# A list scheduler's durations, latencies and load rates replaced, with pauses counted between whole-array and tiled matmuls

## The chip, the cores and the metric

The kernel runs on one core of one Trainium2 chip. The metric is the device time of one execution in microseconds (us), the median of several runs. The engines are TensorE (PE), VectorE (DVE), ScalarE (ACT), GpSimd (POOL) and SyncE (SP, which issues all transfers here). Each takes its own instructions strictly in the order in which the program lists them, and waits for the others through semaphores.

## What is computed

Attention with rotary position codes over 4 batches, 8 heads, 576 positions and head size 64, and behind it a gated network on the 2304 tokens of width 512:

```python
q_rot, k_rot = (rotate(q), rotate(k))
scores = np.matmul(q_rot, k_rot.transpose(0, 1, 3, 2)) / np.sqrt(D)
attn = np.exp(scores - np.max(scores, axis=-1, keepdims=True))
attn = attn / (np.sum(attn, axis=-1, keepdims=True) + 1e-09)
x = np.matmul(attn, v).transpose(0, 2, 1, 3).reshape(B * S, H * D)
...
gate = 1.0 / (1.0 + np.exp(-(x @ w_gate)))      # 512 -> 1536
val = x @ w_val                                  # 512 -> 1536
return (gate * val @ w_out).astype(np.float32)   # 1536 -> 512
```

## The kernel before

Values that need more than 16 bits are held as a scaled float16 and a float16 remainder, and a product is three matmuls of such parts. The eight heads of a batch are four pairs `p`, one head on each half of the 128 partitions. A batch's 576 positions are worked in two halves `i` of 256 and 320 (`HALVES`), with five query tiles `t`: four of 128 and one of 64.

*Attention of batch 0* (`front`, `back`, lines 626 to 723) stays in float32. `front` makes the scores of a tile into a PSUM buffer of the pool `s` (two buffers, taken in turn), and DVE takes their maximum (L645); `back` makes the scores again with the maximum subtracted (L685, L690), ACT takes the exponential (L696), and PE weighs the values and sums (L707); DVE takes a slow reciprocal (L717).

*Attention of batches 1 to 3* (`attention`, `softmax`, `score_mm`, lines 562 to 624 and 725 to 758) works in tiles. PE makes the scores of a pair (batch 1: L572, float32 on half the rows of the array; batches 2 and 3: L584, float16 on the whole array, tile 4 on half the columns). DVE scales them out of PSUM with their extremum (L607), ACT takes the exponential with its sum (L612), two small DVE operations make the reciprocal of the sum (L615, L617), ACT and DVE write the weight as part and remainder (both by helpers, L360 and L366), SP issues a transposing transfer (L738), and when all tiles of a half are there PE multiplies with the values (L748, on half the columns). Rotation of keys and queries is done by DVE for batches 0 and 1 (L514 to L516) and by POOL for 2 and 3 (L521 to L525); for the latter the split keys and queries are copied into `stk` by eight small transfers a pair (L551 to L557).

*The network*: `hidden` (lines 789 to 819) makes, for each of twelve chunks `f` of 128 columns, gate and value by 12 matmuls each (L799), with tanh on ACT (L805) and the product on DVE (L809); `project` (lines 821 to 848) makes 36 matmuls of 512 columns for 128 tokens (L833). Its weights arrive as 64-bit floats and are decoded and split by ACT and DVE in the opening (L366 to L447).

*What sets the order.* Nothing is written in program order. Each step calls `Plan.add` with the engine and its cost in us, a rank, what it reads and writes, and for a transfer a time to landing. `Plan.order` (lines 92 to 201) then plays the program through: at every turn the engine that is free first takes, among the tasks that are ready by then, the one of the lowest rank, whether or not a more urgent one would be ready a little later. A task is ready when its predecessors are done; a result from another engine counts `HOP` later (lines 135 to 143), a transfer its share of one common `bus` and a latency (lines 187 to 190). POOL's tasks and the DVE operations with two SBUF inputs (`op2`) book a common `port` and don't overlap in the plan (lines 184 to 186). The pools `m` and `th` give out a buffer when a task is placed, the others in turn. The tasks are emitted in the order of their planned starts, so each engine's instruction stream is the plan's. Ranks are set in lines 866 to 934: batch `b`'s network has ranks `b` to `b + 1`, the attention of batch `b + 1` from 0.05 less; batch 0's attention starts at -2, the decoding of the input weights at -1.75.

The costs come from four functions (lines 209 to 222) and from constants at the call. A batch's ranks don't depend on them.

Of the kernel before, what the change touches and what calls it, by code (L numbers as in the profile page):

```python
# [58 lines left out]
class Plan:  # L59


    HOP = 0.2
# [5 lines left out]
    def add(self, where, rank, reads, writes, fn, land=0.0, port=False, also=()):  # L68
# [20 lines left out]
        self.tasks.append((where, rank, fn, land, port))  # L89
        self.preds.append(sorted(pre))  # L90

    def order(self):
# [34 lines left out]
        def release(n):  # L127
            for x in self.leases[n]:
                x.left -= 1
                if not x.left:  # L130
                    slots[x.pool][x.n] = max(done[m][1] + done[m][2] for m in x.users) + self.HOP
                    for m in parked.pop(x.pool, []):
                        offer(m)

        def offer(n):
            for e, _ in self.tasks[n][0]:
                t = 0.0
                for m in self.preds[n]:
                    e0, end, land = done[m]
                    t = max(t, end if e0 == e and not land else end + land + self.HOP)  # L140
# [7 lines left out]
        starts, bus, port = [], 0.0, 0.0  # L148
        while len(starts) < N:
# [32 lines left out]
            where, rank, fn, land, locks = self.tasks[n]  # L182
            cost = dict(where)[e]
            if e == "POOL" or (e == "DVE" and locks):
# [24 lines left out]
def c_dve(n, psum=False, two=False):  # L209
    return 0.07 + n / 960 + (0.08 if psum else 0) + (0.15 if two else 0)  # L210


def c_act(n):
    return 0.24 + n * 0.00087


def c_pool(n, two=False):
    return 0.16 + n * (0.0025 if two else 0.0011)


def c_pe(n):
    return n / 2250
# [3 lines left out]
def rope_attention_then_sigmoid_glu(ctx: ExitStack, tc: tile.TileContext, qk, v, w_in, w_out, tables, out):  # L226
# [88 lines left out]
    def mm(us, rank, reads, writes, fn):  # L315
        P.add((("PE", us),), rank, reads, writes, lambda _: fn())

    def tiny(rank, reads, writes, fn, us=0.18):
# [11 lines left out]
    def allmax(rank, src, n, where, reads):  # L330
# [7 lines left out]
        mm(0.15 * n, rank, reads + ["ident"], [Z], turn_up)  # L338
        tiny(rank, [Z], [("row", k)], lambda: V.tensor_reduce(
            out=row[0:1, 2 * k:2 * k + n], in_=at()[0:1, 0:128 * n].rearrange("p (j c) -> p j c", j=n), axis=AX.X,  # L340
            op=ALU.max), us=0.3)
        mm(0.15, rank, [("row", k), "ident"], [Z], lambda: T.matmul(
# [3 lines left out]
    def allsum(rank, src, n, where, reads):  # L346

        at, Z = where
        mm(0.4, rank, reads + ["zero"], [Z], lambda: T.matmul(at()[:, 0:n], lhsT=ones, rhs=src, start=True, stop=True))
# [36 lines left out]
    def w_in_chunk(f, rank):  # L386
# [12 lines left out]
        for g in range(2):  # L399
            op("ACT", c_act(512) + 0.08, rank, tok, [M, W], lambda E, g=g: A.activation(  # L400
# [16 lines left out]
    def w_out_decode(f, rank):  # L417
# [10 lines left out]
        op("ACT", c_act(512) + 0.08, rank, [tok], ["sink", "wob"], lambda E: A.activation(  # L428
# [21 lines left out]
    def values0(rank, step):  # L450
        raw = xt[0].rearrange("p c a n -> p c (a n)").bitcast(F32)
        todo = []
        for p in range(NP):
# [6 lines left out]
            op("ACT", c_act(S) + 0.12, rank, X, ["sink", ("vm", 0)], lambda E, p=p, o=o: A.activation(  # L460
# [18 lines left out]
    def values(b, rank, step):  # L479
# [3 lines left out]
        for p in range(NP):  # L483
            op("ACT", c_act(S) + 0.12, rank, X, ["sink", ("vm", b)], lambda E, p=p: A.activation(
# [11 lines left out]
    def keys_queries(b, p, rank):  # L496
# [34 lines left out]
        for m in range(2):  # L531
            op("ACT", c_act(S) + 0.12, rank, [X[m]], ["sink", M], lambda E, m=m: A.activation(
# [29 lines left out]
    def score_mm(b, p, t, heads, rank):  # L562

        n = slots[b, p][0]
        if b < NW:
            kT, qT = qk0[n][:, 0], qk0[n][:, 1]

            def both(rows, width, to):
# [7 lines left out]
            mm(0.66 * len(heads), rank, R, list(heads),  # L576
               lambda: both(t * 128, 128 if t < 4 else 64, to))
# [12 lines left out]
        else:  # L590
            h = heads[0]
            mm(8 * c_pe(288), rank, R[0] + R[1], [h], lambda: [
                one(e, h()[64 * e:64 * e + 64], 512, 64) for e in range(2)])

    def softmax(b, p, t, u, rank):
# [14 lines left out]
        for c, h in enumerate(heads):  # L610
            op("ACT", c_act(S) + 0.12, rank - 0.01, [("st", k, c)], [prs[c], ("su", k, c)],
# [5 lines left out]
        tiny(rank, [], [("rs", k)], lambda: V.reciprocal(st[:, k, 2, 0:n], st[:, k, 2, 0:n]), us=0.16)  # L617
# [8 lines left out]
    def front(p, i, z, rank):  # L626
# [4 lines left out]
        for x, t in enumerate(((0, 1), (2, 3, 4))[i]):  # L631
            for c in range(2 if t < 4 else 1):
# [10 lines left out]
                mm(0.57 if t < 4 else 1.1, rank, R, [k], direct)  # L643
# [26 lines left out]
    def back(p, i, z, rank):  # L670
# [7 lines left out]
        for j in range(5):  # L678
# [12 lines left out]
            mm(0.0023 * n, rank, R, [k], across)  # L691
# [3 lines left out]
            op("ACT", c_act(2 * n if j < 4 else n), rank - 0.01, [k], [("pt", w, j)],  # L695
# [13 lines left out]
        for js in ((0, 1), (2, 3, 4)):  # L709
            mm(len(js) * 0.0034 * n, rank - 0.02, [("pt", w, j) for j in js] + [("v16", p)], ["pv", U],  # L710
               lambda js=js: weigh(js))
# [5 lines left out]
        op("DVE", 0.1 + 0.0064 * n, rank - 0.02, [], [K], lambda E: V.reciprocal(t(), t()))  # L717
# [7 lines left out]
    def attention(b, p, i, rank, step):  # L725
        n = 0
        z = p % 2 if (b, i) == (0, 0) else i
        for t in ((0, 1), (4, 2, 3) if b % 2 else (2, 3, 4))[i]:
# [9 lines left out]
            transpose(rank, U, [("pt", z, j) for j in range(5)], 2.8 if w == 128 else 1.6, lambda u=u, n=n, w=w: Y.dma_start_transpose(  # L738
# [50 lines left out]
    def hidden(b, f, i, rank):  # L789
# [3 lines left out]
        if i == 0 and b == 0:  # L793
            op("ACT", 0.2, rank, [("vs", b), ("ws", f)], [("gsc", b, f)], lambda E: A.activation(
# [191 lines left out]
```

## Time and profile before

| | |
|---|---|
| median of 3 runs | 716.72 us (716.29 to 717.3) |
| span of the profiled execution, first to last instruction | 719.6 us |
| busy: PE, DVE, ACT, POOL | 672.3 (93%), 482.9 (67%), 437.0 (61%), 73.9 (10%) us |
| weight loads of PE (beside the matmuls) | 426.9 us (59%) |
| mean granted clock of PE | 0.974 of full speed |
| transfers | 89.38 MB, mean 124 GB/s |

The profile records the span of the profiled execution, and no time around it; the span is 2.9 us (0.4%) above the median of the runs without a profile. Busy time of PE is modelled to the end of a matmul's way through the array, so short pauses between two matmuls count as busy. A line of the profile such as L607 is a line of the kernel; L360 and L366 are helpers, told apart there by the tile that they write.

### The profile page before, as it was taken

To read this page: it belongs to the slowest core of one execution; us is meant where nothing else is said; L and a number is where in the kernel's file an instruction comes from. 1 tells how busy PE (TensorE), PEld (TensorE's weight loads), DVE (VectorE), ACT (ScalarE), POOL (GpSimd) and SP (SyncE) were. 2 spreads that over 40 slices of the span, in tenths; PEclk is the share of its full clock that TensorE was granted. 3 is DMA by queue.
4 is the path that set the end of the run, shared out by engine and by line. 5 is a ranking of instruction groups with operands and counts; after the bars stand their busy time and mean duration, and the time that the engine had idled before them with its cause. 6 is when DMAs were issued, how large, how long until landed. Compare 5 with 4: busy or idle time off the path is not lost.

```text
span 719.6 us, 12869 instructions
## 1 busy us (share of the span) xinstructions
PE 672.3 (93%) x4986; PEld 426.9 (59%) x4986; DVE 482.9 (67%) x1062; ACT 437.0 (61%) x885; POOL 73.9 (10%) x57
## 2 busy tenths in 40 slices
PE   1687889999999998998998899999999999999997
PEld 1343455565675455775564665578667756866753
DVE  5677676889888668877797886779938682311310
ACT  2583967796878866665776678577738663322320
POOL 0300000000303001133135001114000000000000
PEclk9996989999999999999998999999999999999999
DMA  9731305226364337664996559764544542000001
GB/s 348 315 125 62 133 41 209 93 92 215 122 163 99 96 96 178 161 165 87 203 210 142 105 126 231 166 159 118 126 110 117 90 109 79 1 15 16 1 15 30
DMA packets 145230, 89.38 MB, mean 124 GB/s; under 512 B 128912, under 2 KB 133648, under 8 KB 143248
## 3 DMA queue, kind: packets, MB, share of 16 engines
q1 hardware_dynamic: 145168, 88.56, 45.7%
q8 instruction: 39, 0.64, 0.4%
q14 instruction: 23, 0.19, 0.1%
HBM read 43.12 MB, written 4.72 MB: 66 GB/s over the span
## 4 chain that ended last, share of the span: by engine, by line
PE 85%; DVE 8%; ACT 3%; DMA 2%; issue 1%; SPq 0%; DVEq 0%; ACTq 0%
PE m L799 37%; PE m L833 20%; PE pv L748 6%; PE s L584 5%; PE s L641 3%; PE s L572 3%; PE pv L707 3%; PE s L690 2%; PE m L707 2%; DVE p L366 1%; PE s L685 1%; DVE p L607 1%; DMA stk<-in_qk_dram 1%; DMA pt<-p 1%; DVE m L645 1%
## 5 line engine op out<-in xcount | busy, mean ns | idle before, releaser
L799 PE MATMUL m<-xt,w 128*128 128x320 f16 (+1 forms) x2304 | 297.1, 287 | 2.3 <-ACT th L805 2.3
L799 PEld LDWEIGHTS <-w 128*128 128x128 f16 x2304 | 221.7, 98 | 74.3 <-issue 18.6
L833 PE MATMUL m<-wo,gt 128*128 128x512 f16 x648 | 146.4, 381 | 0.0
L612 ACT ACTIVATE p<-p,st 128x576 f32<-128x576 f32 x108 | 83.1, 770 | 52.0 <-DVE p L607 45.3
L833 PEld LDWEIGHTS <-gt 128*128 128x128 f16 x648 | 62.4, 98 | 74.2 <-issue 5.0
L366 DVE SCALAR_TENSOR_TENSOR p<-p,st,p 128x576 f16<-128x576 f32 x108 | 91.5, 874 | 20.5 <-ACT p L360 20.2
L809 DVE SCALAR_TENSOR_TENSOR th<-th,m 128x256 f32<-128x256 f32 (+1 forms) x96 | 43.1, 450 | 75.1 <-PE m L799 71.9
L360 ACT ACTIVATE p<-p,st 128x576 f16<-128x576 f32 x108 | 78.3, 763 | 10.6 <-DMA pt<-p 4.5
L360 ACT ACTIVATE gt<-th,c_s 128x256 f16<-128x256 f32 (+1 forms) x96 | 50.5, 529 | 55.2 <-DVE th L809 54.9
L366 DVE SCALAR_TENSOR_TENSOR gt<-th,c_s,gt 128x256 f16<-128x256 f32 (+1 forms) x96 | 56.0, 589 | 19.6 <-ACT gt L360 19.4
L805 ACT ACTIVATE th<-m,gsc 128x256 f32<-128x256 f32 (+1 forms) x96 | 47.3, 494 | 35.1 <-PE m L799 34.5
L607 DVE TENSOR_SCALAR_CACHE_REDUCE p<-s,q_e 128x576 f32<-128x576 f32 x72 | 57.2, 811 | 4.7 <-PE s L584 3.9
L748 PE MATMUL pv<-pt,v 128*64 128x256 f16 (+3 forms) x720 | 54.3, 299 | 0.0
L584 PE MATMUL s<-stk 128*128 128x288 f16 (+1 forms) x320 | 44.9, 290 | 6.4 <-DVE p L607 6.4
L641 PE MATMUL s<-stk 64*128 64x288 f32 (+1 forms) x160 | 33.5, 527 | 18.5 <-DVE stk L516 12.3
L523 POOL TENSOR_TENSOR sw<-sw,tab 128x576 f32<-128x576 f32 x16 | 25.7, 1606 | 225.1 <-DMA sw<-in_qk_dram 225.1
L748 PEld LDWEIGHTS <-v 128*64 128x64 f16 (+1 forms) x720 | 37.3, 113 | 17.6 <-issue 12.8
L521 POOL TENSOR_TENSOR qk<-qk,tab 128x576 f32<-128x576 f32 x16 | 22.8, 1446 | 203.9 <-DMA qk<-in_qk_dram 152.2
L584 PEld LDWEIGHTS <-stk 128*128 128x128 f16 (+1 forms) x320 | 27.2, 100 | 20.0 <-issue 11.9
L645 DVE TENSOR_REDUCE m<-s 128x2 f32<-128x576 f32 x36 | 26.9, 753 | 15.1 <-PE s L641 14.7
L360 ACT ACTIVATE o<-m,o_s 128x512 f32<-128x512 f32 x16 | 10.9, 682 | 41.0 <-PE m L833 40.9
L696 ACT ACTIVATE pt<-s 128x512 f32<-128x512 f32 (+3 forms) x40 | 23.8, 601 | 15.5 <-PE s L690 15.3
(122 smaller groups left out, 700.0 us busy)
## 6 DMA issues: line engine op xcount, KB each, us to landing
wo<-in_w_dram SPq DMA_DIRECT2D x12, 1024.0 KB, 4.8
sw<-in_qk_dram SPq DMA_DIRECT2D x16, 576.0 KB, 5.0
xt<-in_wo_dram SPq DMA_DIRECT2D x12, 512.0 KB, 4.5
stk<-in_qk_dram SPq DMA_DIRECT2D x8, 576.0 KB, 5.0
qk<-in_qk_dram SPq DMA_DIRECT2D x8, 576.0 KB, 5.6
out_dram<-o SPq DMA_DIRECT2D x16, 256.0 KB, 2.1
xt<-in_v_dram SPq DMA_DIRECT2D x3, 1152.0 KB, 6.2
stk<-sw SPq DMA_DIRECT2D x16, 216.0 KB, 3.2
```

The lines of the kernel that those rows point to most:

```text
L360: A.activation(o, src, AF.Copy, scale=scale)
L366: V.scalar_tensor_tensor(out=o, in0=src, scalar=scale, in1=hi, op0=ALU.mult, op1=ALU.subtract)
L584: T.matmul(o[:, c, 0:288], lhsT=q[:, rows:rows + width], rhs=kk[:, c * 288:c * 288 + 288], start=(m == 0), stop=(m == 1))
L607: lambda E, h=h, c=c: V.tensor_scalar(out=prs[c]().rearrange("p (c n) -> p c n", c=2), in0=h()[:, :, 0:288], scalar1=down, scalar2=None, o ...
L612: lambda E, c=c: A.activation(prs[c](), prs[c](), AF.Exp, bias=st[:, k, 0, c:c + 1], scale=-1.0, accum_out=st[:, k, 1, c:c + 1]))
L641: T.matmul(o, lhsT=qT[hs, 128 * t:128 * t + w], rhs=kT[hs, 288 * cc:288 * cc + 288], start=True, stop=True)
L707: T.matmul(o[es, 0:n], lhsT=ones[hs, 0:64] if one else v32[hs, p, j if j == 4 else j + 5 * e], rhs=pp[hs, at0:at0 + n], start=(j == 0), st ...
L748: T.matmul(v_ps[64 * e:64 * e + 64, 0:n], lhsT=v16[hs, p, a, g, :], rhs=pt[z][hs, c * 9 + g, 0:n], start=(first and m == 0), stop=(last an ...
L799: T.matmul(m()[:, 0:n], lhsT=w16[:, f, g, a, cc, :], rhs=x[:, cc, c, c0:c0 + n], start=(k == 0), stop=(k == 11))
L805: op("ACT", c_act(n), rank - 0.05, [m, ("gsc", b, f)], [r], lambda E, m=m: A.activation(t(), m()[:, 0:n], AF.Tanh, scale=gsc[:, b, f:f + 1]))
L809: op("DVE", c_dve(n, psum=True), rank - 0.05, [m], [r], lambda E, m=m: V.scalar_tensor_tensor(out=t(), in0=t(), scalar=1.0, in1=m()[:, 0:n ...
L833: T.matmul(m(), lhsT=gt[:, f, a, c0:c0 + 128], rhs=wo16[:, f, c, :], start=(f == 0 and k == 0), stop=(f == NF - 1 and k == 2))
```

## The change

Every number from which the plan is made is set anew. A result now reaches another engine `TAIL` of its own engine plus `HOP` (0.036) after the planned end, and a dependent operation on the same engine can follow `OWN` later (DVE 0.12, POOL 0.13, else at once). A task of PE may carry a `mode`: `"R"` (matmuls on half of the rows), `"C"` (half of the columns), `"Q"` (both); without one it uses the whole array. Where the mode differs from that of the task placed before it on PE, the start is moved by `ENTER` (from the whole array), `LEAVE` (back to it) or `SWAP`. The mode has no part in choosing the task. What is computed, the ranks, the buffers and the instructions stay as they were.

```diff
-    HOP = 0.2
+    HOP = 0.036
+    TAIL = {"DVE": 0.085, "ACT": 0.1, "POOL": 0.05, "PE": 0.165, "SP": 0.0}
+    OWN = {"DVE": 0.12, "POOL": 0.13}
+    ENTER, LEAVE, SWAP = 0.096, 0.2, 0.25
...
-                    slots[x.pool][x.n] = max(done[m][1] + done[m][2] for m in x.users) + self.HOP
+                    slots[x.pool][x.n] = max(done[m][1] + done[m][2] + self.TAIL[done[m][0]] for m in x.users) + self.HOP
...
-                    t = max(t, end if e0 == e and not land else end + land + self.HOP)
+                    if land:
+                        end += land + self.HOP
+                    elif e0 == e:
+                        end += self.OWN.get(e, 0.0)
+                    else:
+                        end += self.TAIL[e0] + self.HOP
+                    t = max(t, end)
...
             cost = dict(where)[e]
+            if e == "PE":
+                if mode != last:
+                    t += self.ENTER if last is None else self.LEAVE if mode is None else self.SWAP
+                last = mode
...
 def c_dve(n, psum=False, two=False):
-    return 0.07 + n / 960 + (0.08 if psum else 0) + (0.15 if two else 0)
+    return 0.065 + n / 960 + (0.06 if two and n < 600 else 0)
...
 def c_act(n):
-    return 0.24 + n * 0.00087
+    return 0.16 + n * 0.00087
...
 def c_pool(n, two=False):
-    return 0.16 + n * (0.0025 if two else 0.0011)
+    return 0.12 + n * (0.00216 if two else 0.0011)
...
 def c_pe(n):
-    return n / 2250
+    return n / 2400 + 0.0026
...
     def dma(rank, reads, writes, kb, fn, also=()):
-        P.add((("SP", 0.45),), rank, reads, writes, lambda _: fn(), land=(kb / 280, 1.6), also=also)
+        P.add((("SP", 0.5),), rank, reads, writes, lambda _: fn(), land=(kb / (170 if also else 380), 1.4), also=also)
...
     def transpose(rank, reads, writes, us, fn):
-        P.add((("SP", 1.3),), rank, reads, writes, lambda _: fn(), land=(us, 1.2))
+        P.add((("SP", 1.75),), rank, reads, writes, lambda _: fn(), land=(us, 1.0))
...
-    def tiny(rank, reads, writes, fn, us=0.18):
+    def tiny(rank, reads, writes, fn, us=0.085):
...
-            mm(0.66 * len(heads), rank, R, list(heads),
-               lambda: both(t * 128, 128 if t < 4 else 64, to))
+            mm(0.96, rank, R, list(heads), lambda: both(t * 128, 128 if t < 4 else 64, to), mode="R" if t < 4 else "Q")
...
-            op("DVE", c_dve(S, psum=True) + 0.05, rank - 0.01, [h] + Q, [("st", k, c), prs[c]],
+            op("DVE", c_dve(S, psum=True) + 0.02, rank - 0.01, [h] + Q, [("st", k, c), prs[c]],
...
-            op("ACT", c_act(S) + 0.12, rank - 0.01, [("st", k, c)], [prs[c], ("su", k, c)],
+            op("ACT", c_act(S) + 0.09, rank - 0.01, [("st", k, c)], [prs[c], ("su", k, c)],
...
-                mm(0.57 if t < 4 else 1.1, rank, R, [k], direct)
+                mm(0.48 if t < 4 else 0.96, rank, R, [k], direct, mode="R" if t < 4 else "Q")
...
-            mm(0.0023 * n, rank, R, [k], across)
+            mm(0.00215 * n, rank, R, [k], across, mode="R" if j < 4 else "Q")
...
-            transpose(rank, U, [("pt", z, j) for j in range(5)], 2.8 if w == 128 else 1.6, lambda u=u, n=n, w=w: Y.dma_start_transpose(
+            transpose(rank, U, [("pt", z, j) for j in range(5)], 1.3 if w == 128 else 0.8, lambda u=u, n=n, w=w: Y.dma_start_transpose(
...
-            mm(len(js) * 3 * c_pe(n) * 1.1, rank - 0.02, [("pt", z, j) for j in range(5)] + [("v16", p)], ["pv"],
-               lambda js=js: weigh(js, js[0] == 0, js[-1] == 4))
+            mm(len(js) * 3 * c_pe(n) * 1.03, rank - 0.02, [("pt", z, j) for j in range(5)] + [("v16", p)], ["pv"],
+               lambda js=js: weigh(js, js[0] == 0, js[-1] == 4), mode="C")
```

The other call sites change in the same manner: small constants of ACT (0.08 to 0.05, 0.12 to 0.09), the small matmuls of `allmax` and `allsum`, and the mode `"C"` for L707 and for tile 4 of L584.

## Rows read from the trace of the kernel before

**Rows 1.** Windows, six stretches: length, busy PE, PEld, DVE, ACT, POOL, clock, DMA

```profile
0.00:17.00 17.00, 2.40 (x10) 1.30 (x10) 8.78 (x8) 4.90 (x11) 1.31 (x9) 1.00 0.90 344
17.00:108.00 91.00, 73.84 (x480) 40.80 (x481) 64.95 (x128) 57.73 (x109) 5.50 (x4) 0.87 0.36 138
108.00:270.00 162.00, 162.00 (x1179) 96.41 (x1177) 129.18 (x254) 123.77 (x256) 13.36 (x8) 1.00 0.44 132
270.00:414.00 144.00, 133.26 (x1048) 89.17 (x1046) 116.75 (x276) 96.86 (x201) 35.51 (x24) 0.95 0.69 156
414.00:613.00 199.00, 199.00 (x1595) 132.33 (x1592) 140.91 (x350) 127.92 (x263) 18.18 (x12) 1.00 0.55 129
613.00:719.60 106.60, 101.83 (x686) 66.94 (x685) 22.31 (x50) 25.83 (x48) 0.00 (x0) 1.00 0.04 13
```

**Rows 2.** The chain that ended last, its end: start, duration, what

```profile
691.51 23.32 PE m L833 x108
```

**Rows 3.** Windows, one slice of the opening with a low clock

```profile
54.00:72.00 18.00, 13.78 (x70) 7.02 (x72) 13.04 (x28) 5.93 (x13) 0.00 (x0) 0.62 0.19 63
```

**Rows 4.** Waits of PE: for what, us in total, times, longest

```profile
PE s L641 <- DVE stk L516: 12.3, 1, 12.3
PE s L584 <- DVE p L607: 6.4, 5, 2.2
...
PE s L572 <- DVE p L607: 2.0, 1, 2.0
```

**Rows 5.** Timeline, DVE in softmax tiles: start, duration, line, operation, out and in

```profile
291.10 0.16 DVE L615 TENSOR_SCALAR st<-st 128x2 f32<-128x2 f32 x1
291.30 0.17 DVE L617 RECIPROCAL st<-st 128x2 f32<-128x2 f32 x1
291.38 0.74 DVE L607 TENSOR_SCALAR_CACHE_REDUCE p<-s 128x576 f32<-128x576 f32 x1
...
397.69 0.81 DVE L366 SCALAR_TENSOR_TENSOR p<-p,st,p 128x576 f16<-128x576 f32 x1
...
400.08 1.54 DVE L366 SCALAR_TENSOR_TENSOR p<-p,st,p 128x576 f16<-128x576 f32 x2
...
401.80 0.80 DVE L607 TENSOR_SCALAR_CACHE_REDUCE p<-s,q_e 128x576 f32<-128x576 f32 x1
...
402.52 0.82 DVE L607 TENSOR_SCALAR_CACHE_REDUCE p<-s,q_e 128x576 f32<-128x576 f32 x1
```

**Rows 6.** Timeline, ACT: two exponentials of one tile, in square brackets the idle before

```profile
391.09 0.78 ACT L612 ACTIVATE p<-p,st 128x576 f32<-128x576 f32 x1 [1.33 <-DVE p L607]
...
391.87 0.76 ACT L612 ACTIVATE p<-p,st 128x576 f32<-128x576 f32 x1
```

**Rows 7.** The chain that ended last, pieces with and without a change of array

```profile
103.87 0.49 PE s L641 x4
...
229.18 3.99 PE m L833 x18
233.17 1.17 PE s L572 x8
...
582.87 3.88 PE m L833 x18
```

**Rows 8.** Line L738, the transposes: issue in ns and landing in us, minimum, median, maximum

```profile
L738 SPq DMA_TRANSPOSE pt<-p x60: 1285/1888/5836, 204.3 to 596.9; - x60
...
DMA to landing us min/median/max: 3.5/4.0/7.9
```

**Rows 9.** Transfers of the page: line, count, KB each, median us to landing

```profile
sw<-in_qk_dram SPq DMA_DIRECT2D x16, 576.0 KB, 5.0
```

**Rows 10.** Line L615 (ns minimum, median, maximum), and timeline of DVE beside POOL

```profile
L615 DVE TENSOR_SCALAR st<-st x60: 131/164/1378, 193.8 to 593.1; 128x2 f32<-128x2 f32 x48, 128x1 f32<-128x1 f32 x12
...
327.30 3.17 DVE L366 SCALAR_TENSOR_TENSOR gt<-th,c_s,gt 128x256 f16<-128x256 f32 x2
...
328.73 1.46 POOL L525 TENSOR_TENSOR qk<-qk,sw 128x576 f32<-128x576 f32 x1
```

More of the change, by code (lines that the diff above doesn't have):

```diff
@@ L66, in __init__, with add @@
         self.leases = []
-    def add(self, where, rank, reads, writes, fn, land=0.0, port=False, also=()):
+    def add(self, where, rank, reads, writes, fn, land=0.0, port=False, also=(), mode=None):
         n = len(self.tasks)
@@ L88, in add @@
         pre.discard(n)
-        self.tasks.append((where, rank, fn, land, port))
+        self.tasks.append((where, rank, fn, land, port, mode))
         self.preds.append(sorted(pre))
@@ L147, in order @@
                 offer(n)
-        starts, bus, port = [], 0.0, 0.0
+        starts, bus, port, last = [], 0.0, 0.0, None
         while len(starts) < N:
@@ L181, in order @@
                 continue
-            where, rank, fn, land, locks = self.tasks[n]
+            where, rank, fn, land, locks, mode = self.tasks[n]
             cost = dict(where)[e]
+            if e == "PE":
+                if mode != last:
+                    t += self.ENTER if last is None else self.LEAVE if mode is None else self.SWAP
+                last = mode
             if e == "POOL" or (e == "DVE" and locks):
@@ L348, in allsum @@
         at, Z = where
-        mm(0.4, rank, reads + ["zero"], [Z], lambda: T.matmul(at()[:, 0:n], lhsT=ones, rhs=src, start=True, stop=True))
+        mm(0.25, rank, reads + ["zero"], [Z], lambda: T.matmul(at()[:, 0:n], lhsT=ones, rhs=src, start=True, stop=True))
         return lambda: at()[:, 0:n]
@@ L399, in w_in_chunk @@
         for g in range(2):
-            op("ACT", c_act(512) + 0.08, rank, tok, [M, W], lambda E, g=g: A.activation(
+            op("ACT", c_act(512) + 0.05, rank, tok, [M, W], lambda E, g=g: A.activation(
                 dst[:, g, 0], r[:, g], AF.Abs, accum_out=w_m[:, f, g:g + 1]))
@@ L483, in values @@
         for p in range(NP):
-            op("ACT", c_act(S) + 0.12, rank, X, ["sink", ("vm", b)], lambda E, p=p: A.activation(
+            op("ACT", c_act(S) + 0.09, rank, X, ["sink", ("vm", b)], lambda E, p=p: A.activation(
                 sink, raw[:, p], AF.Abs, accum_out=vm[:, b, p:p + 1]))
@@ L531, in keys_queries @@
         for m in range(2):
-            op("ACT", c_act(S) + 0.12, rank, [X[m]], ["sink", M], lambda E, m=m: A.activation(
+            op("ACT", c_act(S) + 0.09, rank, [X[m]], ["sink", M], lambda E, m=m: A.activation(
                 sink, x[:, m], AF.Abs, accum_out=q_m[:, k, m:m + 1]))
@@ L591, in score_mm @@
             h = heads[0]
-            mm(8 * c_pe(288), rank, R[0] + R[1], [h], lambda: [
-                one(e, h()[64 * e:64 * e + 64], 512, 64) for e in range(2)])
+            mm(0.49, rank, R[0] + R[1], [h], lambda: [
+                one(e, h()[64 * e:64 * e + 64], 512, 64) for e in range(2)], mode="C")
     def softmax(b, p, t, u, rank):
@@ L694, in back @@
                 d = d.rearrange("p (e n) -> p e n", e=2)
-            op("ACT", c_act(2 * n if j < 4 else n), rank - 0.01, [k], [("pt", w, j)],
+            op("ACT", c_act(2 * n if j < 4 else n) - 0.11, rank - 0.01, [k], [("pt", w, j)],
                lambda E, j=j, k=k, d=d: A.activation(d, k()[:, :, 0:n] if j < 4 else k()[:, 0, 0:n], AF.Exp,
@@ L709, in back @@
         for js in ((0, 1), (2, 3, 4)):
-            mm(len(js) * 0.0034 * n, rank - 0.02, [("pt", w, j) for j in js] + [("v16", p)], ["pv", U],
-               lambda js=js: weigh(js))
+            mm(len(js) * 0.0035 * n, rank - 0.02, [("pt", w, j) for j in js] + [("v16", p)], ["pv", U],
+               lambda js=js: weigh(js), mode="C")
         K = lease("p32")
@@ L793, in hidden @@
         if i == 0 and b == 0:
-            op("ACT", 0.2, rank, [("vs", b), ("ws", f)], [("gsc", b, f)], lambda E: A.activation(
+            op("ACT", 0.185, rank, [("vs", b), ("ws", f)], [("gsc", b, f)], lambda E: A.activation(
                 gsc[:, b, f:f + 1], w_i[:, f, 0:1], AF.Copy, scale=v_h))
```

18 lines of the change are left out of this document (9 added, 9 removed).

## The prediction

> **What bounds the kernel now.** I read first the busy time of every engine in six stretches of the span [rows 1]. The reader is to see that TensorE (PE) is without a gap in 108 to 270 and in 414 to 613 us: 361 us in which no change of order can give anything back, because nothing waits. The stretch before 17 us is loading, and the last one is matmuls at an even rate up to the final outputs [rows 2]. What can be had lies in two stretches. In 17 to 108 PE is idle for 91.00 - 73.84 = 17.2 us, and in 270 to 414 for 144.00 - 133.26 = 10.7 us. In the same two the granted clock is below 1: 0.87 x 91 and 0.95 x 144, that is 11.8 and 7.2 us of clock that was not granted. The dips follow PE's waits: in 54 to 72 us PE is busy 13.78 of 18 and the mean clock is 0.62 [rows 3], a mixture of its two levels, 1.2 and 2.4 GHz. So at most 17.2 + 10.7 + 11.8 + 7.2 = 46.9 us hang on waits of PE.
>
> Then the list of waits [rows 4]: apart from 12.3 us of first load, the largest entries in which PE stood still are for the scores of a softmax tile whose PSUM buffer VectorE (DVE) had not emptied, L584 and L572, 6.4 + 2.0 = 8.4 us. These are faults of order: PE takes its instructions in the order of the plan, and the plan had thought the buffer free. In 270 to 414 DVE is the busiest engine but PE, 116.75 of 144 us (81%) [rows 1].
>
> **What the change does, part by part.** It adds and removes no instruction. It changes the numbers from which `order` places tasks, so every effect is one of order.
>
> *DVE and ACT.* One softmax tile of two heads costs DVE in the old plan 2 x 0.80 (L607) + 0.18 + 0.16 + 2 x 0.82 (L366) = 3.58 us. The trace, start to start, has 402.52 - 401.80 = 0.72 for L607, 0.20 and 0.08 for the two small operations, and 1.54 - 0.81 = 0.73 for L366 [rows 5]: 2 x 0.72 + 0.28 + 2 x 0.73 = 3.18. The new plan has 2 x 0.685 + 2 x 0.085 + 2 x 0.725 = 2.99, and 0.12 between the two dependent small ones, 3.11. The plan was 13% too long and becomes 2% too short. For the exponential with its sum ACT is planned at 0.861, then at 0.751; the trace has 391.87 - 391.09 = 0.78 [rows 6]. So DVE and ACT move from cover of a tenth to a shortfall of 2 to 4%.
>
> *PE.* Nine matmuls of 512 columns were 2.05 us in the plan and become 1.943; the trace has 23.32 x 9 / 108 = 1.943 [rows 2]. The pauses are real: a visit of eight L572 matmuls among L833 takes 1.17 us where four L641 matmuls of the same shape take 0.49 without a change, so 1.17 - 0.98 = 0.19 for entering, and the 18 L833 after it take 3.99 instead of 3.88, 0.11 for leaving [rows 7]. The new plan writes 0.096 + 0.2 for the same 0.30. The choice of the next task doesn't look at the pause, so none is avoided on purpose. I take 0; if regrouping adds or saves ten visits in the attention of batches 1 to 3 it is 10 x 0.30 = 3 us either way. On balance PE's plan stays about as long as it was (5% less a matmul, the pauses added), while DVE's and ACT's become a tenth shorter: attention is placed earlier against the matmuls of the network.
>
> *DMA.* A transpose was planned at 1.3 + 2.8 + 1.2 + 0.2 = 5.5 us from issue to use and becomes 1.75 + 1.3 + 1.0 + 0.04 = 4.1; in the trace the median is 4.0 and the longest 7.9 [rows 8]. So 1.4 us of cover goes: the longest is then 7.9 - 4.1 = 3.8 us late. On SyncE's queue a transpose now holds 1.75 us in place of 1.3, near the 1.89 of the trace, so what is queued behind (the `stk` writes and the loads) is placed more truly. A load of 576 KB alone goes from 4.3 to 0.5 + 1.52 + 1.4 + 0.04 = 3.5 us, its partner behind it 1.5 later, against a median of 5.0 [rows 9]: the mean of the pair, 4.2, is 0.8 short. What waits for that on its engine is the rotary work on GpSimd (POOL), which has slack, but it then meets DVE where the plan did not put it.
>
> *Sum against the profiled execution (span 719.6 us).* First loads, -0.5 to 0.5, taken as 0: the same DMAs in the same order. Stretch 17 to 108: from an outright 17.2 + 11.8 = 29.0 gain to an equal slip, since a chain of scores, maxima and exponentials through two PSUM buffers is what PE waits for there, and one link of it was priced at 0.57 + 0.2 + 0.75 + 0.2 = 1.72 and is now 0.48 + 0.2 + 0.665 + 0.12 = 1.47, while PE, DVE and ACT all shrink in it alike. I take 0, because a uniform scaling changes no order. Stretch 270 to 414: the waits for the tile, 8.4 us, and the clock that went with them, 7.2 x 8.4 / 10.7 = 5.6; with attention placed earlier DVE has more of it done when the network's matmuls run out. I take all of it, -14.0. Cover lost on the transposes: the longest lateness once, +3.8, because a wait of PE moves all that stands behind it, and the next late transpose finds that time already given. Pauses 0. Together -10.2. The three runs have a median of 716.72, 2.9 below this span; the gain is carried over whole: 716.7 - 10.2 = 706.5 us.
>
> A caution belongs to this sum. Where DVE's operations with two SBUF inputs meet POOL, two L366 take 3.17 us in place of about 1, and the one-input L615 takes up to 1.38 where its median is 0.16 [rows 10]. The plan books POOL and the two-input operations on one `port`; L615 is not among them, and its price goes from 0.18 to 0.085. The Trainium skill, GPSIMD Engine Reference, section Specifications, says that POOL's SBUF interface is shared with VectorE and contends both with two-input operations and with those in a two-port mode. By that rule the new plan has the small operations wrong by more than the old, and the -14.0 would not come; the trace agrees as far as L615's 1.38 us goes.
>
> **The rivals.**
> *The cover was what kept PE fed (slower).* In 414 to 613 PE never waits, with a plan that is late by a tenth on DVE and 1.4 us on each transpose. With exact medians about half of the 24 products of weights and values (three batches, four pairs, two halves) find their last transpose still under way. If the late ones are late by a quarter of the way to the longest, (7.9 - 4.0) / 4 = 1.0 us, PE loses 24 x 0.5 x 1.0 = 12 us if each counts, and the 2% shortfall on DVE's 116.75 us in 270 to 414 adds 2.3. Less a third of the 14.0 that still comes, it is about +9.6: 726. It decides from the point where late landings are not absorbed by the wait before them, as I assumed. For it: the 199 us without a gap; against it: DVE is busy 141 of 199 there and can catch up.
> *The stalls stay.* The collisions at the shared port remain unplanned, the waits move but don't shrink, and the scaling changes little else: 716.7, 715.3 to 718.1. For it: the 3.17 and 1.38 us rows lie in the stretch that stalls.
> *The opening gains too.* If the first network matmuls come earlier because attention 0 and the decoding of weights interlock better, half of the 29.0 goes as well: 706.5 - 14.5 = 692. For it: clock 0.62 in 54 to 72; against it: the chain there is one of latency.
>
> **How the numbers follow.** Forecast, faster by 4 to 17 us, 700 to 713: 0.42. Opening too, 686 to 700: 0.12. No change: 0.12. Slower, 718 to 733: 0.34. The two outer cases are cut at 691 and 729, which leaves about 0.15 out. Where both signs hold so much, the forecast's own range, 700 to 713, stands beside it. A measurement of this kernel tells about 0.2% (1.4 us) from nothing: faster 0.54, same 0.12, slower 0.34.
>
> **What would show it.** Right: in the stretch from 270 to 414 PE busy rises from 133.26 towards 142 and its clock to 1.00, the waits of L584 and L572 for L607 go, and 414 to 613 shows under 4 us of idle PE. Wrong: waits of L748 for `pt` or of L584 for L607 in the last two hundred microseconds of attention, or a granted clock below 1 there (the cover was needed); the same waits at other places (the port). The step I trust least is the 0 for 17 to 108, where the order of some hundred short tasks is dealt anew.

## The result and the profile after

| | before | after |
|---|---|---|
| median | 717.01 us (716.29 to 718.25, 4 runs) | 724.28 us (722.61 to 727.34, 4 runs) |
| span of the profiled execution | 719.6 us | 721.0 us |
| busy: PE, DVE, ACT, POOL | 672.3, 482.9, 437.0, 73.9 us | 671.6, 475.3, 434.7, 76.2 us |
| mean granted clock of PE | 0.974 | 0.981 |

The changed kernel takes 1.0105 times as long, interval 1.0071 to 1.0139: it is slower by 1%, where 706.5 us had been forecast. The lines of the code have moved down by 12 or 13: L799 is now L811, L833 L845, L748 L760, L584 L596, L572 L585, L607 L619, L612 L624, L615 L627, L738 L750, L707 L719, L722 L734.

The profiled execution of after took 722.79 us, 1.8 more than its span. If the same lies around the span of before, that execution took 721.4 us, 4.4 above the median of its kernel, and that of after 1.5 below its own. So the two traces differ by 1.4 us in span and the medians by 7.3; what the traces explain below is the 1.4, as a sum of a gain and two losses, each larger.

The same six stretches as in [rows 1], for after (length, busy PE, PEld, DVE, ACT, POOL, clock, DMA share, GB/s):

```profile
0.00:17.00 17.00, 4.06 (x14) 1.77 (x14) 9.11 (x9) 4.90 (x11) 1.31 (x9) 1.00 0.88 329
17.00:108.00 91.00, 73.95 (x481) 41.08 (x480) 71.93 (x142) 68.15 (x131) 7.40 (x4) 0.89 0.48 177
108.00:270.00 162.00, 155.79 (x1130) 94.08 (x1127) 115.10 (x234) 110.71 (x231) 13.23 (x8) 0.98 0.37 109
270.00:414.00 144.00, 140.41 (x1158) 93.91 (x1157) 123.58 (x301) 105.43 (x219) 30.39 (x20) 1.00 0.74 164
414.00:613.00 199.00, 194.09 (x1514) 128.70 (x1513) 133.56 (x333) 119.02 (x246) 23.83 (x16) 1.00 0.55 126
613.00:721.00 108.00, 103.24 (x700) 68.19 (x697) 22.01 (x45) 26.45 (x50) 0.00 (x0) 1.00 0.04 13
```

The reader is to see three things against [rows 1]. In 270 to 414 PE is busy 140.41 us in place of 133.26, at a clock of 1.00 in place of 0.95. In 108 to 270, where PE had been without a gap, it is now idle for 162.00 - 155.79 = 6.2 us and the clock is 0.98. In 414 to 613 it is idle for 4.9 us where it had not been idle at all. To put one measure on busy time and clock, I added up, for every matmul of each trace, the time that it needs at full clock (an estimate from its columns): by 180 us both kernels have done the same, by 270 after is 8.0 us behind, by 414 it is 3.8 ahead, and from 594 on it is 1.4 behind, which is the difference of the spans. So 11.8 was gained in 270 to 414, and 8.0 and 5.2 were lost on either side of it.

The largest waits of PE in 270 to 414, after (in us, times, longest); the same list of before has L584 and L572 for L607 with 6.4 + 2.0 [rows 4]:

```profile
PE s L596 <- DVE p L619: 1.7, 3, 1.1
PE pv L760 <- DMA pt<-p: 1.0, 1, 1.0
```

And in 414 to 613, where before has no wait:

```profile
PE pv L760 <- DMA pt<-p: 2.8, 3, 1.8
PE s L596 <- DVE p L619: 1.3, 4, 0.5
PE s L596 <- DMA stk<-sw: 0.5, 1, 0.5
```

The 8.0 us of the first loss fall into one slice of 18 us. Before, then after:

```profile
180.00:198.00 18.00, 18.00 (x134) 12.41 (x133) 15.64 (x31) 14.43 (x31) 7.20 (x4) 1.00 0.36 122
```

```profile
180.00:198.00 18.00, 13.99 (x75) 7.63 (x72) 12.80 (x32) 13.81 (x32) 5.89 (x4) 0.81 0.46 158
```

After has 4.0 us without PE, and 0.19 x 18 = 3.4 us of clock that was not granted. The timeline of PE there, after (start, duration, line, operation, in brackets the idle before and what ended it):

```profile
183.31 0.70 PE L719 MATMUL m<-pt,ones 64*64 64x320 f32 x4
183.95 1.24 PE L585 MATMUL s<-stk 64*128 64x288 f32 x8
188.34 0.58 PE L362 MATMUL m<-wo_m,ones 128*128 128x1 f32 x2 [3.15 <-DVE wo_m L447]
188.85 2.44 PE L585 MATMUL s<-stk 64*128 64x288 f32 x8
191.22 3.38 PE L811 MATMUL m<-xt,w 128*128 128x320 f16 x12
194.54 0.59 PE L350 MATMUL pv<-ident,xm 128*1 128x128 f32 x2
195.06 1.80 PE L811 MATMUL m<-xt,w 128*128 128x320 f16 x12
```

PE stands for 3.15 us, and the eight L585 and twelve L811 that come next take 2.44 and 3.38 us where eight and twelve take 1.24 and 1.80 at other times: half the clock, after the pause. The instruction at which PE stands, L362, belongs to the scale of the output weights and waits for their maximum (`wo_m`, L447); in before the same instruction comes at 210.4, and PE doesn't stand for it. Behind it there was little else to do, because network work is missing. The matmuls with 256 columns are those of the first half of batch 0. After has done its last twelve by 172.8, while before still has 48 of them for the time in which the attention ends. After, then before:

```profile
171.29 1.48 PE L811 MATMUL m<-xt,w 128*128 128x256 f16 x12
```

```profile
177.29 5.41 PE L799 MATMUL m<-xt,w 128*128 128x256 f16 x48
```

The matmuls with 320 columns are those of the second half, and they need the end of its attention. In after the first of them start at 191.22, in before at 183.81:

```profile
183.81 1.80 PE L799 MATMUL m<-xt,w 128*128 128x320 f16 x12
```

The last operation of that attention as a line of its own (minimum, median, maximum in ns, first and last start), before and after:

```profile
L722 DVE TENSOR_REDUCE xm<-xt x8: 407/444/480, 51.1 to 182.9; 128x1 f32<-128x256 f16 x4, 128x1 f32<-128x320 f16 x4
```

```profile
L734 DVE TENSOR_REDUCE xm<-xt x8: 410/442/480, 50.3 to 190.7; 128x1 f32<-128x256 f16 x4, 128x1 f32<-128x320 f16 x4
```

It comes 7.8 us later. Pieces of the chain of waits through 165 to 215 us, after, show how its last steps are strung on the decoding of the output weights (`xt`, `wo` and `sink` here) and the transfer that feeds it:

```profile
172.92 0.56 ACT xt L385
...
174.79 4.72 DMA xt<-in_wo_dram
...
179.60 0.69 ACT xt L385
180.29 0.57 ACT xt L390
180.86 0.90 ACT pt L708 x2
...
185.05 2.06 DVE p L729
```

The exponential L708 of the attention stands behind L385 in ACT's stream, and L385 stands behind a load: it starts at 179.60, when the load has landed, and L708 at 180.86.

### The profile page after: what moved, and what is told of

The parts are those of the page before. It is cut to its first block, busy times and chain, and to the rows that moved or that the text cites. A ratio compares the mean times of both kernels' runs of the same rounds, so it can differ in the third digit from the quotient of the medians.

```text
span 721.0 us, 12857 instructions
## 1 busy us (share of the span) xinstructions
PE 671.6 (93%) x4986; PEld 427.7 (59%) x4986; DVE 475.3 (66%) x1062; ACT 434.7 (60%) x885; POOL 76.2 (11%) x57
## 4 chain that ended last, share of the span: by engine, by line
PE 52%; DVE 21%; ACT 13%; DMA 9%; issue 5%; SPq 0%; ACTq 0%; DVEq 0%
PE m L811 23%; PE m L845 15%; DMA pt<-p 6%; DVE p L379 4%; PE pv L760 4%; DVE p L619 3%; ACT p L373 3%; ACT p L624 2%; PE s L585 2%; DVE m L657 2%; PE s L653 2%; DVE p L729 2%; PE s L596 1%; DMA xt<-in_wo_dram 1%; DVE wo L394 1%
## 5 line engine op out<-in xcount | busy, mean ns | idle before, releaser
L811 PE MATMUL m<-xt,w 128*128 128x320 f16 (+1 forms) x2304 | 296.1, 287 | 1.5 <-DVE th L821 1.4
L811 PEld LDWEIGHTS <-w 128*128 128x128 f16 x2304 | 223.1, 98 | 70.6 <-issue 14.3
L845 PE MATMUL m<-wo,gt 128*128 128x512 f16 x648 | 146.1, 379 | 0.0
L624 ACT ACTIVATE p<-p,st 128x576 f32<-128x576 f32 x108 | 83.0, 769 | 57.9 <-DVE p L619 53.2
L845 PEld LDWEIGHTS <-gt 128*128 128x128 f16 x648 | 61.6, 98 | 73.4 <-issue 5.0
L373 ACT ACTIVATE p<-p,st 128x576 f16<-128x576 f32 x108 | 78.2, 763 | 10.7 <-DMA pt<-p 4.7
L619 DVE TENSOR_SCALAR_CACHE_REDUCE p<-s,q_e 128x576 f32<-128x576 f32 x72 | 57.1, 810 | 0.4 <-PE s L596 0.4
L760 PE MATMUL pv<-pt,v 128*64 128x256 f16 (+3 forms) x720 | 51.5, 288 | 4.7 <-DMA pt<-p 4.4
L760 PEld LDWEIGHTS <-v 128*64 128x64 f16 (+1 forms) x720 | 36.7, 109 | 20.6 <-issue 13.4
L534 POOL TENSOR_TENSOR qk<-qk,tab 128x576 f32<-128x576 f32 x16 | 25.0, 1583 | 218.0 <-DMA qk<-in_qk_dram 116.8
L596 PE MATMUL s<-stk 128*128 128x288 f16 (+1 forms) x320 | 44.5, 287 | 3.6 <-DVE p L619 3.0
L596 PEld LDWEIGHTS <-stk 128*128 128x128 f16 (+1 forms) x320 | 26.9, 100 | 16.9 <-issue 10.3
L653 PEld LDWEIGHTS s<-stk 64*128 64x128 f32 (+1 forms) x160 | 14.6, 210 | 32.0 <-DVE m L657 12.3
L619 DVE TENSOR_SCALAR_CACHE_REDUCE p<-s 128x576 f32<-128x576 f32 x36 | 26.7, 750 | 7.2 <-PE s L585 7.1
```

What stands on the lines that cost most here:

```text
L373: A.activation(o, src, AF.Copy, scale=scale)
L534: either(places, rank, gate, X[m], lambda E, m=m: E.tensor_tensor(out=x[:, m], in0=x[:, m], in1=tab[:, 0], op=ALU.mult))
L596: T.matmul(o[:, c, 0:288], lhsT=q[:, rows:rows + width], rhs=kk[:, c * 288:c * 288 + 288], start=(m == 0), stop=(m == 1))
L619: lambda E, h=h, c=c: V.tensor_scalar(out=prs[c]().rearrange("p (c n) -> p c n", c=2), in0=h()[:, :, 0:288], scalar1=down, scalar2=None, o ...
L624: lambda E, c=c: A.activation(prs[c](), prs[c](), AF.Exp, bias=st[:, k, 0, c:c + 1], scale=-1.0, accum_out=st[:, k, 1, c:c + 1]))
L653: T.matmul(o, lhsT=qT[hs, 128 * t:128 * t + w], rhs=kT[hs, 288 * cc:288 * cc + 288], start=True, stop=True)
```

## The experiments

The change was cut into four groups of numbers: *loads* (the costs of plain transfers), *transposes*, *PE* (its durations and the pauses) and *engines* (durations of DVE, ACT and POOL, and the latencies `HOP`, `TAIL`, `OWN`). Together they are the whole change. Where the engines' group is undone and a transfer's not, or the reverse, the 0.164 us by which `HOP` differs is put into the transfer's landing, so that the landing stays as it was. Every ratio is to runs of before on the same chip, whose medians were 717.5 to 718.3. A trace is of one execution, which can lie some us from the median of its kernel: that of the loads' run took 733.16 us for 724.25, that of the first run without the engines' numbers 703.41 for 708.21.

**One group undone at a time.** First the loads, then the transposes:

```diff
-... land=(kb / (170 if also else 380), 1.4), also=also)   # SP 0.5
+... land=(kb / 280, 1.764), also=also)                    # SP 0.45
```

> The changed kernel with one group of its numbers as before: the cost of plain transfers (0.45 us of issue, 280 KB per us, landing 1.6 us and the old hop). All else is the change's. Loads theory: the 8 us that the changed kernel loses at 180 to 198 us come from loads that are planned to land in 3.3 us and land in 4.7 us, so ScalarE stands behind a load; with the old landing the loss goes, 716 +- 2 us. Cover theory (the engines' and transposes' tighter costs took PE's slack): 724 +- 2, nothing changes. Scatter theory (any order dealt anew lands within some 1%): anything from 710 to 730, without regard to what is undone.

Measured: 724.25 us, 1.0070 (1.0052 to 1.0089). Undoing the loads' numbers moves the time by nothing that is clear of the intervals, and the 716 of the loads theory didn't come.

```diff
-... (("SP", 1.75),) ... land=(us, 1.0)     # us = 1.3, 0.8
+... (("SP", 1.3),) ... land=(us, 1.364)    # us = 2.8, 1.6
```

> The changed kernel with the transposes' cost as before (1.3 us of issue, 2.8 and 1.6 on the bus, 1.2 to landing and the old hop). Cover theory: the 4.4 us in which PE stood before the products of weights and values for a transpose go, 720 us. Loads theory: 724 +- 2. Scatter theory: 710 to 730.

Measured: 721.94 us, 1.0047 (1.0030 to 1.0065). With the old cover PE is busy 185.17 of 186 us in 414 to 600 (after: 181.09), so the 5 us of waits there were the lost cover; but 270 to 414 falls to 135.11, and the time moves by only 2.3 (about 4 where each is held against before on its own chip).

```diff
-    ENTER, LEAVE, SWAP = 0.096, 0.2, 0.25
+    ENTER, LEAVE, SWAP = 0.0, 0.0, 0.0
-    return n / 2400 + 0.0026
+    return n / 2250
...
```

> The changed kernel with PE's durations as before and no pause for a change of array. Cover theory and loads theory: 724 +- 2, since PE's plan stays equally long. Pause theory (pauses delay PE in the plan and let DVE and ACT run into idle time): 717. Scatter theory: 710 to 730.

Measured: 722.58 us, 1.0055 (1.0036 to 1.0074). Undoing durations and pauses together moves the time by 1.7 us, though 270 to 414 falls from 140.41 to 133.67 us of PE.

```diff
-    HOP = 0.036
+    HOP = 0.2        # TAIL all 0.0, OWN empty
-    return 0.065 + n / 960 + (0.06 if two and n < 600 else 0)
+    return 0.07 + n / 960 + (0.08 if psum else 0) + (0.15 if two else 0)
-    return 0.16 + n * 0.00087
+    return 0.24 + n * 0.00087
...
```

> The changed kernel with the durations of DVE, ACT and POOL and the latencies between engines as before (transfers land after the same time as in the change). Cover theory: the tenth of cover on DVE and ACT comes back, the small waits of PE between 414 and 613 us go, 718 +- 2. Loads theory: 724 +- 2. Scatter theory: 710 to 730.

Measured: 708.21 us, 0.9838 (0.9803 to 0.9873). This group is what makes the change slow: without it the same change is 1.6% faster than before. PE is busy 160.95 of 162 in 108 to 270 and the stall at 180 is gone.

**The engines' group split**, durations alone or latencies alone as before:

```diff
-    return 0.16 + n * 0.00087
+    return 0.24 + n * 0.00087
...
```

> The changed kernel with the durations of DVE, ACT and POOL as before; latencies between engines, transfers and PE are the change's. Cover theory (it is the tenth of length on each operation that keeps the engines from standing behind each other): as fast as with all of the engines' numbers undone, 708 +- 3. Latency theory (the shorter hop does it): 722 +- 3. Scatter theory: 705 to 730, without regard to what is undone.

```diff
-    HOP = 0.036
+    HOP = 0.2        # TAIL all 0.0, OWN empty
```

> The changed kernel with the latencies between engines as before (one hop of 0.2 us, nothing between two dependent operations of one engine); durations, transfers and PE are the change's. Cover theory: 722 +- 3, the durations are still short. Latency theory: 708 +- 3. Scatter theory: 705 to 730.

Measured: old durations 712.44 us, 0.9923 (0.9896 to 0.9950); old latencies 729.55, 1.0161 (1.0127 to 1.0194). The two are not additive: old durations give back 12 us, old latencies cost 5, both together give back 16. So in this one draw of each it is the new durations that cost, and neither half alone reaches 708. With the old latencies and the new durations the attention of batch 0 ends at 201.2 us, the list of waits of PE in 108 to 270 begins thus, and PE is busy 150.45 of 162:

```profile
PE m L673 <- DVE cb L668: 8.2, 2, 6.3
```

L673 and L668 belong to that attention too.

**Is it chance?** A greedy order can change much on a small number. I call one set of the plan's numbers, with the order that comes of it, a draw. So the cost of a DVE operation was raised by 1 ns, in before and in the version with the engines' numbers undone:

```diff
-    return 0.07 + n / 960 + ...
+    return 0.071 + n / 960 + ...
```

> The kernel before with 1 ns more on every DVE operation of the plan (0.070 to 0.071): no theory of costs gives this any effect, but ties and near ties in the plan fall otherwise. Cover, latency and loads theories: 717 +- 1.5. Scatter theory: it moves by as much as the change did, 5 us or more either way.

> The fast kernel of the first four (engines' numbers as before, transfers and PE as in the change) with 1 ns more on every DVE operation of the plan. Cover theory: 708 +- 2. Scatter theory: most of the gain goes again, 714 or more.

Measured: before 728.23 us, 1.0151 (1.0118 to 1.0184); the other 702.47, 0.9797 (0.9763 to 0.9832). One nanosecond makes before slower by 1.5%, more than the whole change does. The waits in 270 to 414 grow (before with 1 ns more):

```profile
PE s L584 <- DVE p L607: 6.8, 4, 2.9
PE m L799 <- ACT th L805: 4.3, 1, 4.3
PE s L572 <- DVE p L607: 4.1, 2, 3.8
```

To see which of the two kernels is the unusual one, the changed kernel was drawn twice more (0.066 and 0.067 in place of 0.065) and before once more (0.072 in place of 0.07):

> The changed kernel with 1 ns more on every DVE operation of the plan (0.065 to 0.066). Since 1 ns took the kernel before from 717 to 728, the question is how wide the changed kernel scatters. Cover theory (short costs of DVE, ACT and POOL make it slower, on top of a scatter): it stays slow, 718 to 732. Scatter alone: 702 to 730, as likely below 717 as above.

> The changed kernel with 2 ns more on every DVE operation of the plan. Cover theory: 718 to 732. Scatter alone: 702 to 730.

> The kernel before with 2 ns more on every DVE operation of the plan. If 717 was a lucky draw of its costs: 722 to 732 again. If the 728 was the unlucky one: 714 to 720.

Measured: the changed kernel 723.73, 1.0099 (1.0063 to 1.0136), and 726.24, 1.0111 (1.0079 to 1.0142); before 726.95, 1.0122 (1.0107 to 1.0137). The changed kernel stands at 724 to 726 in three draws. Before stands at 717, 728 and 727: its own numbers are a lucky draw, by 10 us against both neighbours. Against these two neighbours the change is not slower: its ratios of 1.0099 to 1.0111 stand beside their 1.0122 and 1.0151, which makes it 1 to 4 us faster, not clear of the intervals.

**Is it cover?** Cover is what a plan has where its durations are longer than the real ones. The rival of the prediction said that durations a tenth too long had kept PE fed. The changed kernel with the costs of DVE, ACT and POOL a tenth longer in the plan, nothing else:

```diff
-            cost = dict(where)[e]
+            cost = dict(where)[e] * (1.1 if e in ("DVE", "ACT", "POOL") else 1.0)
```

> The changed kernel with every duration of DVE, ACT and POOL in the plan times 1.1; the small operations and the latencies between engines as in the change. Cover theory: a tenth of cover is most of what the old durations had, 705 to 714. Scatter alone: 702 to 730.

Measured: 730.63 us, 1.0178 (1.0150 to 1.0206). Cover as an even margin does not help; 108 to 270 becomes emptier still (148.91 us of PE), and attention of batch 0 ends at 204.6. That rival falls in this form.

**One group alone, on top of before.** PE's durations and pauses; the pauses without the durations; the transfers alone; the engines' numbers alone:

```diff
-    return n / 2250
+    return n / 2400 + 0.0026
+    ENTER, LEAVE, SWAP = 0.096, 0.2, 0.25
...
```

> The kernel before with one group of the change alone: PE's durations and the pauses. Two-stages theory: PE's numbers are what fills 270 to 414 us (PE busy 133 to 140 there) and the short durations of DVE and ACT are what empties 108 to 270 (162 to 156); so here 270 to 414 fills and 108 to 270 stays full: 702 to 710. Transfers theory (the new landing times of transposes and loads fill 270 to 414): nothing is gained, 717 to 728. Scatter theory: 702 to 730, with no link to the stages.

```diff
+    ENTER, LEAVE, SWAP = 0.096, 0.2, 0.25
```

> The kernel before with the pauses for a change of array alone, PE's durations as they were. If it is the pauses that fill 270 to 414: 702 to 712 and over 137 us of PE there. If it is the shorter matmuls: 717 to 728 and under 134. Scatter theory: 702 to 730.

```diff
-... land=(kb / 280, 1.6), also=also)      # transposes as well
+... land=(kb / (170 if also else 380), 1.236), also=also)
```

> The kernel before with the numbers of the transfers alone (the fast kernel with PE's numbers undone). Two-stages theory: 270 to 414 stays empty, 127 to 134 us of PE there, 717 to 728. Transfers theory: 702 to 710, over 137. Scatter theory: 702 to 730.

```diff
-    HOP = 0.2
+    HOP = 0.036      # TAIL, OWN and the durations of the change
```

> The kernel before with the durations of DVE, ACT and POOL and the latencies between engines alone. Two-stages theory: it has the loss and not the gain, 722 to 735; PE under 158 us in 108 to 270 or under 134 in 270 to 414. Theory that only the mixture hurts: 714 to 720. Scatter theory: 702 to 730.

Measured: PE's numbers 729.98 us, 1.0166 (1.0122 to 1.0211); pauses alone 708.09, 0.9875 (0.9838 to 0.9913); transfers alone 714.46, 0.9941 (0.9911 to 0.9971), with runs from 708 to 717; engines' numbers alone 728.29, 1.0163 (1.0117 to 1.0209). The engines' numbers cost 10 us on before as it is, and 16 to 22 in the change. But before is the lucky draw: beside its neighbours (728.2, 727.0) the 728.29 shows no cost, so only the runs on the change, two draws without the group (708.2, 702.5) against three with it (724 to 726), show one. The transfers' 714.46 lies between what either theory had said. PE's numbers alone had been expected at 702 to 710 by the theory of two stages, which falls with the 730. The pauses alone are worth 9.7 us. Counted in matmuls at full clock most of it, about 10 us of the 14 by which the two traces differ, is earned in 270 to 414, most of the rest before 108. Before with the pauses alone:

```profile
270.00:414.00 144.00, 140.11 (x1164) 95.91 (x1164) 124.33 (x288) 102.60 (x214) 35.47 (x24) 0.99 0.71 160
```

That is the 140 of the whole change (after: 140.41), without any of its durations. The engines' numbers alone bring 136.65 at a clock of 0.99, the transfers alone 137.52 at 0.99. With PE's true durations beside the pauses the same stretch has 130.84 us and L585 waits for L619 again, for 4.1 us (before with PE's numbers):

```profile
PE s L585 <- DVE p L619: 4.1, 2, 3.8
PE s L596 <- DVE p L619: 3.9, 2, 2.4
PE m L811 <- ACT th L817: 3.2, 1, 3.2
```

Since before itself had been a lucky draw, both were drawn again with 0.071:

> The kernel before with the pauses alone, and 1 ns more on every DVE operation of the plan: a second draw of the same numbers. If the pauses bring the gain by themselves: 704 to 712 and over 137 us of PE in 270 to 414, as without the 1 ns. If the 708 was the draw: 715 or more.

> The kernel before with the pauses and PE's durations, and 1 ns more on every DVE operation of the plan: a second draw. If the shorter matmuls take back what the pauses bring as long as the transfers are as before: 724 to 734 and under 134 us of PE in 270 to 414. If the 730 was the draw: 715 or less.

Measured: pauses alone 709.18, 0.9894 (0.9849 to 0.9939); PE's numbers 728.81, 1.0158 (1.0115 to 1.0201). The two differ by 20 to 22 us in either draw, and the pauses are worth 8.5 us against before, or 19 against before with the same 0.071 (728.23). Beside that 728.23 PE's numbers cost nothing: its durations take away what the pauses bring.

**A version that beats both.** The change without the engines' group: 708.21 us, and 702.47 with 1 ns more, 0.9797 of before. The stretches of the latter (17 to 108, 108 to 270, 270 to 414):

```profile
17.00:108.00 91.00, 76.26 (x538) 41.96 (x536) 70.72 (x141) 67.68 (x128) 5.52 (x4) 0.94 0.43 163
108.00:270.00 162.00, 161.92 (x1181) 96.62 (x1180) 125.76 (x256) 119.16 (x247) 12.34 (x8) 1.00 0.42 127
270.00:414.00 144.00, 141.22 (x1167) 97.38 (x1166) 128.63 (x301) 104.72 (x221) 36.55 (x24) 1.00 0.77 169
```

Against before the opening and the stall are both better and the middle is as full. Counted in matmuls at full clock, this version is 6.7 us ahead of before by 108 us (without the 1 ns it was 9.9), as far by 270, and 21 by 414. Its attention of batch 0 ends at 173.2:

```profile
L734 DVE TENSOR_REDUCE xm<-xt x8: 410/448/480, 46.1 to 173.2; 128x1 f32<-128x256 f16 x4, 128x1 f32<-128x320 f16 x4
```

**What orders the kernels.** The last start of that line (L722 or L734), against the median time, for all twenty kernels that have a profile: the nine in which it comes at 188 us or later (188.3 to 204.6) all take 721.9 to 730.6 us. Of the eleven in which it comes at 187.3 or before, seven take 702.5 to 717. The other four lose it later: PE is idle in 270 to 600 for 19 us in before with 1 and with 2 ns more and in the change with PE's numbers undone, and for 14.6 us in PE's numbers with 1 ns more, where the seven fast ones have 4.2 to 10.7. Attention of batch 0 over in time, and PE fed from 270 on: the two conditions together separate all twenty. The bounds were set afterwards, with 187.3 and 188.3 next to each other, and traces are held against medians: it is a sorting of twenty traces, not a proof of cause.

A second sorting is wider. Between the start of the last matmul of 256 columns and that of the first of 320 lie 18.5 to 27.1 us in seven kernels: the change in its three draws, the change with the loads' or the transposes' numbers undone, that with the tenth of cover, and the engines' numbers alone. In the other thirteen it is at most 5.7. From 180 to 198 the seven do 9.2 to 10.6 us of matmuls at full clock, the others 12.8 to 17.7. All seven have the new numbers of the engines, though two others that have the new durations (PE's numbers undone, old latencies) show no such gap. By these rows what empties the stretch in the seven is that the network of the first half runs out long before the attention of the second half ends.

## Why the prediction was wrong

**The step that failed** is the sentence of the first part that 108 to 270 and 414 to 613 are "361 us in which no change of order can give anything back". That is right for gains and was used as if it held for losses: the sum has no term for 108 to 270 at all. Counted in matmuls at full clock, none of the twenty traces gains more than half a microsecond on before in either stretch. But the change lost 8.0 us in the first, nearly all of it between 180 and 198: the attention of batch 0 ended 7.8 us later, the network of its first half had been done 10 us earlier (172.8 for 182.7), and that of its second half could not start. A stretch without a gap should have been priced as a risk: which task, made late, would empty it. The trace of before had the answer. Its network matmuls of 320 columns begin at 183.81, right behind the last L722 at 182.9, and what PE had for the time before were 48 matmuls of the first half, 5.4 us.

**270 to 414, -14.0.** Right in place, and near in size: 11.8 came, the clock rose to 1.00, and the waits for L619 fell from 8.4 to 1.7. The cause given was at best a part. The prediction had it from DVE's truer durations and "pauses 0". On before, each of three groups alone fills the stretch: counted in matmuls at full clock, the engines' numbers by about 6 us, the transfers' by 8, the pauses by 10; PE's durations beside the pauses undo it (130.84 us of PE), and 1 ns on before takes 7 away. How the 11.8 divide in the change is not shown. The term for the pauses was mis-sized where they stand alone: 0 (within 3 us) in the sum, 8.5 and 9.7 us in the runs. In the change they come with PE's durations, and the two undone together moved the time by 1.7. I had asked only whether the plan would avoid pauses. That they put PE later in the plan's time against DVE and ACT is how I read it, and not shown.

The price of leaving a tiled visit (0.11 us) holds, though its row was misread. The 18 L833 of [rows 7] don't follow the visit of L572: nine others and two small matmuls stand between. The nine right behind it take 2.05 us for 1.943, the same 0.11:

```profile
226.83 2.05 PE m L833 x9
```

**Lost cover on the transposes, +3.8.** Right: 4.9 us of idle PE in 414 to 613, 2.8 of it for `pt`, and nearly all gone with the old cover. "Once only" was an underestimate: three waits, the longest 1.8.

**17 to 108, 0.** Right here: the work done by 108 differs by less than 1 us. It was not a safe zero, since over the kernels tried it runs from 1.8 us less than before to 9.9 more.

**The time of before.** The sum was made against a profiled execution 4.4 us slower than the median by the estimate above, and its gain carried over whole. A gain of 10.2 on a trace that shows rarer stalls may be less on a usual run; no trace of a usual run of before exists, so how much of the remaining 5.9 us (7.3 - 1.4) lies there is open. Before was also a lucky draw, which no row of its trace could tell: that the result has the sign of a loss hangs on it, that the forecast gain of 10.2 didn't come doesn't, since the change is at most some 4 us faster than the neighbours of before.

**The signs.** Busy PE, clock and waits in 270 to 414 came as the signs of being right had said, in a kernel that became slower; 414 to 613 shows 4.9 us of idle PE where under 4 was asked. The signs had nothing on 108 to 270, as the sum had not.

**The rivals.** The one called "the cover was what kept PE fed" gave 726, close to 724.3, but by another way: it put the loss into late transposes (12) and DVE (2.3) with only a third of the 14.0 gained. The gain came nearly whole, the transposes cost 5, and 8 were lost where it looked for nothing; and an even cover of a tenth made things worse. "The stalls stay" fell with the waits of 270 to 414; the caution's conclusion, that the -14.0 would not come, fell with it. The Trainium skill, GPSIMD Engine Reference, section Specifications, has POOL's SBUF interfaces shared with VectorE, with contention for two-input operations and for those in a two-port mode. The trace of after agrees so far as the small operation L627 still shows the long case beside POOL (1265 ns, where 1378 was the longest [rows 10]). "The opening gains too" did not happen in after; it did in the fast versions, by about 2 us (pauses alone with 1 ns more) to 9.9 (the engines' numbers undone).

**Open.** Why plans with the true durations of DVE and ACT end the attention of batch 0 later and use up the network of its first half sooner. In after eleven of the twelve chunks of output weights are taken up by ACT before the last exponential of that attention, in before six; but before with the pauses alone has eleven as well, and its attention ends at 179.8. The chain shows the last links, ACT behind a load of the output weights, but ACT waits for that load in the fast versions as well, 5.7 us in all in the fastest, so the load is not by itself the cause. Nor was it tried whether another rank for the decoding would give the same gain.

## What to carry to other kernels

A stretch in which the bounding engine never waits is not a zero in the sum: ask how much work is in stock there, and how late a task has to be to use it up. Before believing 1% from a change of a greedy plan's numbers, move one number by a nanosecond in both kernels and time again: here that alone was worth 10 us, and one of the two kernels compared was a lucky draw. Set such numbers group by group and time each: the truest durations were not the best, and three groups without the fourth gained 1.6 and 2.0% in two draws where all four lost 1%.

## What the runs showed of the hardware

Nothing that contradicts the rows of before. A pause of PE of 3.15 us was followed by eight L585 and twelve L811 at half the clock (2.44 us for 1.24 and 3.38 for 1.80), so that it cost 3.15 + 1.20 + 1.58 = 5.9 us, about twice its length. The transposes' issue on SP stayed at a median of 1.89 us.
